# Fixing TensorE's order in the attention loop, and moving the preparation of six weight pieces into its first half

## The chip, the cores and the metric

The kernel runs on one core of a Trainium2 chip. The metric is device time in microseconds (us). Before the change it is 664.98 us, the median of three runs that lie between 664.54 and 666.16 us.

The engines go by the profile's names: PE is TensorE (matrix products and transposes), PEld its weight loads, DVE is VectorE, ACT is ScalarE, POOL is GpSimd, SP is SyncE, which here issues the DMAs.

## The reference

The program is an attention stage followed by two blocks on its result.

```
scores = q @ k.T / 8, kept where q and k have the same nearest centroid   # 2 batches x 8 heads, 768 x 768, depth 64
x = softmax(scores) @ v                                                   # -> [2, 768, 512]
h = relu(x.T @ w_tok1) @ w_tok2          # token weights: 768 x 256 and 256 x 768
u = x + h.T
x = u + relu(u @ w_ch1) @ w_ch2          # 512 -> 1536 -> 512
theta = x @ w_theta
y = w_tok_r @ (x * cos(theta)) + w_tok_i @ (x * sin(theta))
out = (x + y) + relu((x + y) @ w_ch)
```

Weights and the activations of the later blocks are split in a high and a low part, and a product takes three matmuls (L126, L127, L128).

## The kernel before

**Units.** Attention is 48 units: 16 heads times three pairs of 128-row query tiles. The loop at L485 issues in step n the scores of unit n, the turn of unit n-1 and the values of unit n-2.

- Scores (L380 to L407): eight matmuls, four for each of two query tiles, into one of two `ps_s` buffers a tile. DVE takes the negated row maximum (nm, L400), ACT the exponential (e, L402); this frees the `ps_s` buffer.
- Turn (L409 to L424): twelve 128 x 128 transposes into three `ps_t` tiles, the only three buffers that `ps_t` has. ACT copies two of them to SBUF (p, L420), DVE the third (L422).
- Values (L426 to L449): six matmuls, recorded in the trace as twelve, into `ps_o`, which has one buffer. ACT copies one half (tmp, L445), DVE adds the other (xt, L447); only then is the buffer free for the next unit's values.

**Work beside the units.** Six units are a pair of heads. For each next pair there are cluster masks (sim L246, pp L270, oh L271, m L286; sim and pp go through `ps_t`), and POOL splits the pair's q and k (`split_pair`: L346, L80, L86). After each pair `natural` (L451 to L467) turns its result into rows: six transposes x (L460) into two `ps_t` tiles, and six DVE products xn (L462). Below, an x-unit is a unit in which these x transposes stand.

**The six weight pieces.** `load_w` (L100 to L120) brings one piece of 128 x 512: a DMA on SP's queue, two ACT instructions (L109, L110), two on DVE (L112, L113), one on POOL (L116), and then the high part by POOL (L80) or ACT (L84) and the low part by POOL or DVE (L86). Its last argument names the engines: "pp" is POOL for both, "av" is ACT and DVE, "pv" POOL and DVE. w_tok1 has three pieces, issued in steps 41, 43 and 46 (`W1_AT`); w_tok2 has three, issued in step 48, behind the last tmp and p.

**Behind the attention** (called the tail here): `tok_up` of batch 0 (18 matmuls g for each of two halves, L126 to L128; then gh by ACT L147 and gl by DVE L148), the split of batch 1's rows (xh by ACT L84, xl by DVE L86), and `tok_down` of batch 0 (h, L126 to L128).

**What sets the order.** Every engine runs its queue in order. The queues are filled by a scheduler that simulates a timeline (L799) and picks among the instructions that are ready; `tc.issue_after(x)` adds that an instruction stands behind x in its own engine's queue. Where the program names no such order, the scheduler has interleaved scores, transposes and values of neighbouring units.

Of the kernel before, what the change touches and what calls it, by code (L numbers as in the profile page):

```python
# [31 lines left out]
HL = 4  # L32

X_AT = (29, 31, 33, 35, 37, 39)
W1_AT = {41: "pp", 43: "pp", 46: "av"}
PREP = (1, 0)
PACE = 2
TH0 = 6
# [11 lines left out]
def tile_model(ctx: ExitStack, tc: tile.TileContext, qT, kT, v, cent, w1, w2, wc1, wc2, wth, wri, wch, out):  # L50


    nc = tc.nc
    B, H, D, S = qT.shape
    NT = S // P
# [12 lines left out]
    marks = {}  # L68
# [61 lines left out]
    w1s, w2s, xs, gs = [], [], {}, {}  # L130
# [30 lines left out]
    with ExitStack() as actx:  # L161
# [218 lines left out]
        def scores(b, h, u, ops):  # L380

            qh, ql, k1, kk, _ = ops
            es = []
            for j in range(2):
                qt = 2 * u + j
                c = slice(qt * P, qt * P + P)
                ps = ps_s.tile([P, 2, 512], F32, tag="s", name=f"s{b}{h}{qt}")
                first = (b, h, u) == (0, 0, 0)
                if first:

                    for half in range(2):
                        nc.tensor.matmul(ps[:, half, :NH], qh[:, c], k1[:, half * NH : half * NH + NH], start=True, stop=False)
                with tc.issue_after(marks["cl"].ins) if first else nullcontext():
                    for half in range(2):
                        n = slice(half * NH, half * NH + NH)
                        if not first:
                            nc.tensor.matmul(ps[:, half, :NH], qh[:, c], k1[:, n], start=True, stop=False)  # L397
                        marks["scores"] = nc.tensor.matmul(ps[:, half, :NH], ql[:, c], kk[:, n], start=False, stop=True)  # L398
                nm = small.tile([P, 1], F32, tag="nm", bufs=4, name=f"nm{b}{h}{qt}")
                marks["max"] = nc.vector.tensor_reduce(out=nm, in_=ps[:, :, :NH], axis=AX.XY, op=ALU.max, negate=True)  # L400
                e = ap.tile([P, S], F32, tag="e", bufs=4, name=f"e{b}{h}{qt}")
                marks["exp"] = nc.scalar.activation(  # L402
                    out=e.rearrange("p (a n) -> p a n", a=2), in_=ps[:, :, :NH], func=AF.Exp,
                    bias=nm, accum_out=sums[b, h // 2][:, qt, h % 2 : h % 2 + 1],
                )
                es.append(e)
            return es  # L407

        def turn(b, h, u, es):  # L409

            pr = []
            for j in range(NT // 2):
                ps = ps_t.tile([P, 2, 256], F32, tag="t", name=f"t{b}{h}{u}{j}")
                for i in range(2):
                    for a in range(2):
                        kt = 2 * j + a
                        marks["turn"] = nc.tensor.transpose(ps[:, a, i * P : i * P + P], es[i][:, kt * P : kt * P + P], ident)  # L417
                p = ap.tile([P, 2, 256], F32, tag="p", bufs=PB, name=f"p{b}{h}{u}{j}")
                if KINDS[j] == "A":
                    marks["pA"] = nc.scalar.activation(out=p, in_=ps, func=AF.Copy)  # L420
                else:
                    marks["pV"] = nc.vector.tensor_copy(out=p, in_=ps)  # L422
                pr.append(p)
            return pr  # L424

        def values(us):  # L426


            if us[-1][0] == len(units) - 1:
                ps = ps_s.tile([P, 2, 512], F32, tag="s", name="olast")[:, 0, :]  # L430
            else:
                ps = ps_o.tile([P, 512], F32, tag="o", name=f"o{us[0][0]}")
            outs = []
            for i, (n, pr, vs) in enumerate(us):
                po = ps[:, 256 * i : 256 * i + 256]
                for kt in range(NT):
                    r = 64 * (kt % 2)
                    nc.tensor.matmul(  # L438
                        po[r : r + 64, :], vs[:, kt, :], pr[kt // 2][:, kt % 2, :], start=kt < 2, stop=kt >= NT - 2,
                        tile_position=(0, r),  # L440
                    )
                outs.append((units[n], po))
            for (b, h, u), po in outs:
                tmp = ap.tile([64, 256], F32, tag="tmp", bufs=2, name=f"tmp{b}{h}{u}")
                marks["tmp"] = nc.scalar.activation(out=tmp, in_=po[64:128, :], func=AF.Copy)  # L445
                r0 = 64 * (h % 2)
                nc.vector.tensor_tensor(  # L447
                    out=xts[b, h // 2][r0 : r0 + 64, u * 256 : u * 256 + 256], in0=po[0:64, :], in1=tmp, op=ALU.add
                )  # L449
# [25 lines left out]
        with tc.issue_after(marks["cst"].ins):  # L475
            ops = {heads[0]: prep_pair_first(raws) + (vs00,)}
# [5 lines left out]
        units = [(b, h, u) for b, h in heads for u in range(NT // 2)]  # L482
        es, prs = {}, {}
        late, group = [], []
        for n in range(len(units) + SKEW):  # L485
            if n < len(units):
                b, h, u = units[n]
                if u == 0 and h % 2 == 0:
                    sums[b, h // 2] = small.tile([P, NT, 2], F32, tag="sm", bufs=2, name=f"sm{b}{h}")
                    xts[b, h // 2] = ap.tile([P, S], F32, tag="xt", bufs=2, name=f"xt{b}{h}")  # L490
                if n != 1:
                    es[n] = scores(b, h, u, ops[b, h])
                if n == 0:
                    next(first, None)
                    place(1, ms[0, 0])
                    scored = marks["scores"]
                    es[1] = scores(*units[1], ops[b, h])
                    with tc.issue_after(marks["max"].ins):
                        ops[heads[1]] = prep_first(*heads[1])
                    marks["scores"] = scored  # L500
                    for w, k in zip(WARM[1:], ("cps", "sim", "scores")):
                        with tc.issue_after(marks[k].ins):
                            warm_up(w)
                h1 = n // 3 + 1
                if 1 < h1 < len(heads) and u == PREP[h1 % 2]:
                    b2, h2 = heads[h1]
                    ops[b2, h2] = prep(b2, h2, ms[b2, h2 // 2])
                p1 = n // 6 + 1
                if p1 < len(heads) // 2:
                    pr = heads[2 * p1][0], heads[2 * p1][1] // 2  # L510
                    if n % 6 == PAIR_AT[0]:
                        raws = load_pair(*pr)
                    if n % 6 == PAIR_AT[1]:
                        split_pair(*pr, raws)
                    if n % 6 == PAIR_AT[2]:
                        gen = masks(*pr)
            if n >= 3:
                for _ in range(PACE):
                    next(gen, None)
            if n == 42:  # L520
                mctx.close()
            if 0 <= n - 1 < len(units):
                prs[n - 1] = turn(*units[n - 1], es.pop(n - 1))
            if n < 3:
                with tc.issue_after((marks["turn"] if n else marks["scores"]).ins):
                    for _ in range(PACE):
                        next(gen, None)
            if 0 <= n - SKEW:
                b, h, u = units[n - SKEW]
                group.append((n - SKEW, prs.pop(n - SKEW), ops[b, h][4]))  # L530
                if len(group) == GROUP:
                    with tc.issue_after(marks["turn"].ins):
                        values(group)
                    group = []
                if h % 2 == 1 and u == NT // 2 - 1:
                    late.append((n + 1, b, h // 2))
            while late and (n >= late[0][0] or n == len(units) + SKEW - 1):
                _, b, pr = late.pop(0)
                natural(b, pr)
            if n in X_AT:  # L540
                tok_x(0, X_AT.index(n), part, "pp")
            if n in W1_AT:
                with tc.issue_after(marks["exp"].ins):
                    i = len(w1s)
                    w1s.append(load_w(w1[:, i * 512 : i * 512 + 512], f"w1_{i}", W1_AT[n]))
            if n == len(units):
                with tc.issue_after(marks["tmp"].ins), tc.issue_after(marks["pA"].ins), tc.issue_after(marks["pV"].ins):
                    for i in range(NT // 2):
                        w2s.append(load_w(w2[:, :, i * 256 : i * 256 + 256], f"w2_{i}", "pv"))


        ps = ps_s.tile([P, 2, 512], F32, tag="s", name="g0")
# [194 lines left out]
    for n in range(len(steps) + 2):  # L747
        if n < len(steps):
            t, b = steps[n]
# [53 lines left out]
```

## Time and profile before

| | |
|---|---|
| median of 3 runs | 664.98 us |
| the profiled execution's own time | 664.99 us |
| span of the profiled execution | 663.3 us |
| mean granted TensorE clock | 0.995 |
| PE busy | 646.8 us, 98% |
| DVE busy | 401.2 us, 60% |
| ACT busy | 344.9 us, 52% |
| POOL busy | 257.6 us, 39% |

The span runs from the first to the last instruction; 1.7 us of the execution lie outside it. Attention takes the first 245 us or so, the two blocks the rest. A start-to-start difference between two PE rows is the time that PE's queue really took for what lies between them; the busy time of a row is longer where matmuls overlap.

### The profile page before, as it was taken

The numbers are of one execution on the slowest core, as the hardware profiler recorded it, in microseconds if no ns is written. First come the engines' busy times: TensorE is split into PE (matmuls) and PEld (weight loads), VectorE is DVE, ScalarE is ACT, GpSimd is POOL, SyncE is SP. The second block draws the span as 40 slices with busy tenths as digits, with TensorE's granted clock in tenths as the row PEclk, the third lists the DMA queues.
The fourth block names the chain that finished last, engine by engine and source line by source line (L and its number), as shares of the span: only waits on it lengthen the run. The fifth ranks groups of instructions, "written<-read, shape, count | busy, mean of one in ns | idle before, by whom it ended". The sixth has DMA issues, their size and how long they took to land.

```text
span 663.3 us, 9795 instructions
## 1 busy us (share of the span) xinstructions
PE 646.8 (98%) x3591; PEld 517.7 (78%) x3591; DVE 401.2 (60%) x649; ACT 344.9 (52%) x653; POOL 257.6 (39%) x231
## 2 busy tenths in 40 slices
PE   7999999999999989999999999999999999999998
PEld 4777777777777758878888888888887878888886
DVE  5877778687787776466665442546677694531212
ACT  5676776777767863256444320428487673320000
POOL 6230312364031131138887520603467796541000
PEclk9999999999999998999999999999999999999999
DMA  8554755444555121023433310310021424300001
GB/s 294 160 138 105 169 123 144 120 117 114 113 123 124 37 96 47 18 67 124 154 133 127 126 53 14 95 33 0 1 85 42 128 88 127 114 20 33 16 33 47
DMA packets 24207, 61.42 MB, mean 93 GB/s; under 512 B 4256, under 2 KB 7520, under 8 KB 24160
## 3 DMA queue, kind: packets, MB, share of 16 engines
q1 hardware_dynamic: 24160, 60.80, 32.3%
q8 instruction: 28, 0.46, 0.3%
q14 instruction: 19, 0.16, 0.1%
HBM read 39.65 MB, written 3.15 MB: 65 GB/s over the span
## 4 chain that ended last, share of the span: by engine, by line
PE 86%; ACT 4%; DVE 3%; POOL 3%; issue 2%; DMA 2%; SPq 0%; POOLq 0%; ACTq 0%
PE o L438 10%; PE t L417 9%; PE s L397 5%; PE r L126 5%; PE r L127 5%; PE r L128 5%; PE c L126 5%; PE c L127 5%; PE c L128 5%; PE s L398 5%; PE y L128 4%; PE y L127 4%; PE y L126 4%; PE po L126 2%; PE po L128 2%
## 5 line engine op out<-in xcount | busy, mean ns | idle before, releaser
L402 ACT ACTIVATE e<-s,nm 128x768 f32<-128x768 f32 x96 | 86.7, 905 | 29.4 <-DVE nm L400 28.1
L400 DVE TENSOR_REDUCE nm<-s 128x1 f32<-128x768 f32 x96 | 90.5, 951 | 18.9 <-PE s L398 18.0
L417 PE MATMUL t<-ident,e 128*128 128x128 f32 x576 | 80.5, 275 | 0.6 <-ACT p L420 0.5
L417 PEld LDWEIGHTS t<-ident,e 128*128 128x128 f32 x576 | 66.4, 140 | 16.0 <-issue 9.4
L397 PE MATMUL s<-k,qh 128*128 128x384 f32 x188 | 71.9, 382 | 2.5 <-ACT e L402 2.3
L438 PE MATMUL o<-p,vs 128*64 128x256 f32 x564 | 71.2, 388 | 0.0
L398 PE MATMUL s<-k,q 128*128 128x384 f32 x192 | 65.3, 343 | 2.4 <-DVE q L279 2.4
L420 ACT ACTIVATE p<-t 128x512 f32<-128x512 f32 x96 | 52.2, 594 | 25.4 <-PE t L417 25.0
L126 PE MATMUL r<-ul,c_h 128*128 128x512 f32 x144 | 56.5, 396 | 0.4 <-DVE ul L90 0.4
L126 PE MATMUL y<-zl,k_h 128*128 128x512 f32 x144 | 56.1, 390 | 0.0
L128 PE MATMUL y<-zh,k_h 128*128 128x512 f32 x144 | 56.1, 390 | 0.0
L127 PE MATMUL r<-uh,c_l 128*128 128x512 f32 x144 | 56.1, 390 | 0.0
L127 PE MATMUL y<-zh,k_l 128*128 128x512 f32 x144 | 56.0, 389 | 0.0
L127 PE MATMUL c<-c_h,rl 128*128 128x512 f32 x144 | 56.0, 390 | 0.0
L128 PE MATMUL r<-uh,c_h 128*128 128x512 f32 x144 | 56.0, 390 | 0.0
L128 PE MATMUL c<-c_h,rh 128*128 128x512 f32 x144 | 55.9, 390 | 0.0
L126 PE MATMUL c<-c_l,rh 128*128 128x512 f32 x144 | 55.2, 391 | 0.0
L438 PEld LDWEIGHTS o<-p,vs 128*64 128x64 f32 x564 | 36.3, 136 | 22.7 <-issue 5.9
L116 POOL TENSOR_TENSOR c_f<-c_f,c_raw 128x512 uint32<-128x512 uint32 x24 | 31.6, 1318 | 44.7 <-issue 31.3
L80 POOL TENSOR_SCALAR qh<-ql 128x768 fp32r<-128x768 f32 x7 | 5.8, 835 | 100.9 <-DMA qh<-qh 100.8
L397 PEld LDWEIGHTS s<-k,qh 128*128 128x128 f32 x188 | 35.4, 188 | 11.1 <-ACT e L402 5.6
L398 PEld LDWEIGHTS s<-k,q 128*128 128x128 f32 x192 | 36.7, 192 | 3.8 <-ACT k L276 3.4
(192 smaller groups left out, 1387.9 us busy)
## 6 DMA issues: line engine op xcount, KB each, us to landing
c_raw<-wc SPq DMA_DIRECT2D x24, 512.0 KB, 3.3
k_raw<-wri SPq DMA_DIRECT2D x18, 512.0 KB, 3.5
qh<-qh SPq DMA_DIRECT2D x28, 192.0 KB, 3.0
k<-kh SPq DMA_DIRECT2D x28, 192.0 KB, 3.8
ql<-qT SPq DMA_DIRECT2D x8, 384.0 KB, 3.2
kl<-kT SPq DMA_DIRECT2D x8, 384.0 KB, 4.6
vs<-v SPq DMA_DIRECT2D x16, 192.0 KB, 2.4
w_raw<-w SPq DMA_DIRECT2D x6, 512.0 KB, 4.1
```

Source lines behind the costliest of these rows:

```text
L80: nc.gpsimd.tensor_scalar(out=h, in0=x, scalar1=1.0, scalar2=0.0, op0=ALU.mult, op1=ALU.add)
L116: nc.gpsimd.tensor_tensor(out=wu, in0=wu, in1=lo, op=ALU.add)
L126: nc.tensor.matmul(ps, ah, bl, start=first and i == 0, stop=False)
L127: nc.tensor.matmul(ps, al, bh, start=False, stop=False)
L128: nc.tensor.matmul(ps, ah, bh, start=False, stop=last and i == n - 1)
L397: nc.tensor.matmul(ps[:, half, :NH], qh[:, c], k1[:, n], start=True, stop=False)
L398: marks["scores"] = nc.tensor.matmul(ps[:, half, :NH], ql[:, c], kk[:, n], start=False, stop=True)
L400: marks["max"] = nc.vector.tensor_reduce(out=nm, in_=ps[:, :, :NH], axis=AX.XY, op=ALU.max, negate=True)
L402: marks["exp"] = nc.scalar.activation(out=e.rearrange("p (a n) -> p a n", a=2), in_=ps[:, :, :NH], func=AF.Exp, bias=nm, accum_out=sums[b, ...
L417: marks["turn"] = nc.tensor.transpose(ps[:, a, i * P : i * P + P], es[i][:, kt * P : kt * P + P], ident)
L420: marks["pA"] = nc.scalar.activation(out=p, in_=ps, func=AF.Copy)
L438: nc.tensor.matmul(po[r : r + 64, :], vs[:, kt, :], pr[kt // 2][:, kt % 2, :], start=kt < 2, stop=kt >= NT - 2, tile_position=(0, r),)
```

## The change

There are two parts. The first gives PE a fixed order in attention: the scores of unit n stand behind the last values matmul issued so far (unit n-3), and the transposes of unit n-1 stand behind the scores of unit n. The values stood behind the transposes already. The second issues the six weight pieces in steps 8, 12, 16, 20, 24 and 28, first the three of w_tok1, then those of w_tok2, each behind an exponential on ACT, and all with "pp".

```diff
-W1_AT = {41: "pp", 43: "pp", 46: "av"}
+W_AT = (8, 12, 16, 20, 24, 28)
...
-                    nc.tensor.matmul(
+                    marks["o"] = nc.tensor.matmul(
...
                 if n != 1:
-                    es[n] = scores(b, h, u, ops[b, h])
+                    with tc.issue_after(marks["o"].ins) if "o" in marks else nullcontext():
+                        es[n] = scores(b, h, u, ops[b, h])
...
-                prs[n - 1] = turn(*units[n - 1], es.pop(n - 1))
+                with tc.issue_after(marks["scores"].ins) if n > 2 else nullcontext():
+                    prs[n - 1] = turn(*units[n - 1], es.pop(n - 1))
...
-            if n in W1_AT:
+            if n in W_AT:
                 with tc.issue_after(marks["exp"].ins):
-                    i = len(w1s)
-                    w1s.append(load_w(w1[:, i * 512 : i * 512 + 512], f"w1_{i}", W1_AT[n]))
-            if n == len(units):
-                with tc.issue_after(marks["tmp"].ins), tc.issue_after(marks["pA"].ins), tc.issue_after(marks["pV"].ins):
-                    for i in range(NT // 2):
-                        w2s.append(load_w(w2[:, :, i * 256 : i * 256 + 256], f"w2_{i}", "pv"))
+                    i = W_AT.index(n)
+                    if i < NT // 2:
+                        w1s.append(load_w(w1[:, i * 512 : i * 512 + 512], f"w1_{i}", "pp"))
+                    else:
+                        i -= NT // 2
+                        w2s.append(load_w(w2[:, :, i * 256 : i * 256 + 256], f"w2_{i}", "pp"))
```

PE's queue in steps 10 and 11 of the loop, before. s034 and s035 are the scores of unit 11, t0310 to t0312 the transposes of unit 10, o8 the values of unit 8; "x2" is two instructions in a row.

```order
L397 MATMUL s034_871<-k103_568,qh03_567 128x384
L398 MATMUL s034_871<-k2_1_152,q2_1_150 128x384
L397 MATMUL s034_871<-k103_568,qh03_567 128x384
L398 MATMUL s034_871<-k2_1_152,q2_1_150 128x384
L438 MATMUL o8_861<-p0220_782,vs02_465 64x256 x2
L438 MATMUL o8_861<-p0221_789,vs02_465 64x256 x2
L438 MATMUL o8_861<-p0222_796,vs02_465 64x256 x2
L417 MATMUL t0310_889<-ident_61,e032_815 128x128 x2
L417 MATMUL t0311_896<-ident_61,e032_815 128x128 x2
L417 MATMUL t0312_903<-ident_61,e032_815 128x128 x2
L397 MATMUL s035_880<-k103_568,qh03_567 128x384
```

The same place of PE's queue after the change:

```order
L438 MATMUL o8_873<-p0222_808,vs02_465 64x256 x2
L397 MATMUL s034_883<-k103_568,qh03_567 128x384
L398 MATMUL s034_883<-k2_1_152,q2_1_150 128x384
L397 MATMUL s034_883<-k103_568,qh03_567 128x384
L398 MATMUL s034_883<-k2_1_152,q2_1_150 128x384
L397 MATMUL s035_892<-k103_568,qh03_567 128x384
L398 MATMUL s035_892<-k2_1_152,q2_1_150 128x384
L397 MATMUL s035_892<-k103_568,qh03_567 128x384
L398 MATMUL s035_892<-k2_1_152,q2_1_150 128x384
L417 MATMUL t0310_901<-ident_61,e032_827 128x128 x2
L417 MATMUL t0310_901<-ident_61,e033_836 128x128 x2
```

The values moved ahead of both score tiles, and the transposes no longer stand between the two score tiles.

DVE's queue in unit 17 (query tiles s054 and s055), before. o14 are the values of unit 14, p0502 and p0512 the third copies of the turns of units 15 and 16.

```order
L400 TENSOR_REDUCE nm053_1195<-s053_1190 128x1
L422 COPY p0502_1232<-t0502_1227 128x512
L400 TENSOR_REDUCE nm054_1249<-s054_1244 128x1
L447 TENSOR_TENSOR xt04_921<-o14_1234,tmp042_1241 64x256
L400 TENSOR_REDUCE nm055_1258<-s055_1253 128x1
L422 COPY p0512_1281<-t0512_1276 128x512
```

The same unit after; w1_2 is the third piece of w_tok1.

```order
L400 TENSOR_REDUCE nm053_1219<-s053_1214 128x1
L422 COPY p0502_1256<-t0502_1251 128x512
L400 TENSOR_REDUCE nm054_1285<-s054_1280 128x1
L112 TENSOR_SCALAR w1_2_raw_1268<-w1_2_f_1270 128x512
L400 TENSOR_REDUCE nm055_1294<-s055_1289 128x1
L447 TENSOR_TENSOR xt04_933<-o14_1258,tmp042_1265 64x256
L113 SCALAR_TENSOR_TENSOR w1_2_f_1270<-w1_2_f_1270,w1_2_raw_1268 128x512
L422 COPY p0512_1317<-t0512_1312 128x512
```

The piece's two DVE instructions came in, and the addition xt, which frees `ps_o`, moved from between the two maxima to behind both.

ACT's queue behind the last tmp (the tail), before. gh00 and gh01 are the two halves of `tok_up` of batch 0, xh10 to xh15 the six tiles of batch 1, w2_2 the last piece of w_tok2, c1_0 the first of the next block's weights.

```order
L147 ACTIVATE gh00_3286<-g0_3267 128x512
L109 ACTIVATE w2_2_f_3230<-w2_2_raw_3228 128x512
L84 ACTIVATE xh10_3312<-xn6_72 128x512
L84 ACTIVATE xh11_3316<-xn7_73 128x512
L147 ACTIVATE gh01_3308<-g0_3267 128x512
L84 ACTIVATE xh12_3320<-xn8_74 128x512
```

The same place after:

```order
L147 ACTIVATE gh00_3286<-g0_3267 128x512
L84 ACTIVATE xh10_3312<-xn6_72 128x512
L84 ACTIVATE xh11_3316<-xn7_73 128x512
L84 ACTIVATE xh12_3320<-xn8_74 128x512
L84 ACTIVATE xh13_3324<-xn9_75 128x512
L84 ACTIVATE xh14_3328<-xn10_76 128x512
L84 ACTIVATE xh15_3332<-xn11_77 128x512
L109 ACTIVATE c1_0_f_3598<-c1_0_raw_3596 128x512
L110 ACTIVATE c1_0_raw_3596<-c1_0_raw_3596 128x512
L147 ACTIVATE gh01_3308<-g0_3267 128x512
```

The second half's gh01 moved from behind two of the six xh to behind all six and behind two instructions for c1_0. From there on the queues of all engines hold the same instructions in the same order before and after.

## Rows read from the trace of the kernel before

**Rows 1.** The page, busy time of TensorE (us, share of the span, instructions).

```profile
PE 646.8 (98%) x3591; PEld 517.7 (78%) x3591; DVE 401.2 (60%) x649; ACT 344.9 (52%) x653; POOL 257.6 (39%) x231
```

**Rows 2.** The chain of waits through attention: start, duration (us), what; values only.

```profile
51.87 1.45 PE o L438 x12
58.64 1.45 PE o L438 x12
62.97 1.45 PE o L438 x12
...
108.04 1.45 PE o L438 x12
...
202.76 1.45 PE o L438 x12
...
235.37 1.45 PE o L438 x12
```

**Rows 3.** Timeline of PE, a unit already in the new order: start, duration, instruction.

```profile
139.28 0.47 PE L397 MATMUL s<-k,qh 128*128 128x384 f32 x1
...
140.80 1.47 PE L417 MATMUL t<-ident,e 128*128 128x128 f32 x12
142.20 1.52 PE L438 MATMUL o<-p,vs 128*64 128x256 f32 x12
```

**Rows 4.** Timeline of all engines in an x-unit; brackets: idle time before, and releaser.

```profile
109.42 0.44 PE L397 MATMUL s<-k,qh 128*128 128x384 f32 x1
...
110.42 0.96 DVE L400 TENSOR_REDUCE nm<-s 128x1 f32<-128x768 f32 x1 [1.65 <-PE s L398]
...
111.63 1.26 DVE L462 TENSOR_TENSOR xn<-x,ri 128x128 f32<-128x128 f32 x6
...
112.52 0.44 PE L397 MATMUL s<-k,qh 128*128 128x384 f32 x1 [0.62 <-ACT e L402]
...
113.28 1.80 DVE L400 TENSOR_REDUCE nm<-s 128x1 f32<-128x768 f32 x2
```

**Rows 5.** Timeline of all engines where a weight piece is prepared in attention.

```profile
217.49 0.69 ACT L109 ACTIVATE w_f<-w_raw 128x512 f32<-128x512 f32 x1
...
218.66 0.42 DVE L112 TENSOR_SCALAR w_raw<-w_f 128x512 uint32<-128x512 uint32 x1
...
220.12 0.42 DVE L447 TENSOR_TENSOR xt<-o,tmp 64x256 f32<-64x256 f32 x1
...
220.57 0.69 DVE L113 SCALAR_TENSOR_TENSOR w_f<-w_f,w_raw 128x512 uint32<-128x512 uint32 x1
```

**Rows 6.** Timeline of the tail, all engines.

```profile
245.77 0.60 ACT L147 ACTIVATE gh<-g 128x512 fp32r<-128x512 f32 x1 [2.34 <-PE g L128]
245.78 1.69 DVE L86 TENSOR_TENSOR w_l<-w_f,w_h 128x512 fp32r<-128x512 f32 x2
...
247.79 0.68 DVE L148 SCALAR_TENSOR_TENSOR gl<-g,gh 128x512 fp32r<-128x512 f32 x1
...
248.52 0.50 PE L126 MATMUL g<-xl,w_h 128*128 128x512 f32 x1 [2.57 <-DVE gl L148]
...
249.06 0.63 ACT L84 ACTIVATE xh<-xn 128x512 fp32r<-128x512 f32 x1 [1.49 <-PE g L126]
...
254.34 0.39 PE L126 MATMUL h<-gl,w_h 128*128 128x512 f32 x1
```

**Rows 7.** Windows: stretch; its length, busy PE, PEld, DVE, ACT, POOL; PEclk, DMA share, GB/s.

```profile
250.00:252.00 2.00, 2.00 (x6) 1.51 (x6) 0.19 (x1) 0.63 (x1) 1.69 (x2) 0.50 0.00 0
...
500.00:520.00 20.00, 18.36 (x89) 14.99 (x88) 15.48 (x24) 13.59 (x25) 15.43 (x13) 1.00 0.25 79
```

**Rows 8.** Timelines of POOL and DVE: a pair's split, and a weight piece in the tail.

```profile
157.44 1.84 POOL L86 TENSOR_TENSOR kl<-kl,kh 128x768 fp32r<-128x768 f32 x1 [0.51 <-DMA k<-kl]
...
241.74 1.33 POOL L116 TENSOR_TENSOR w_f<-w_f,w_raw 128x512 uint32<-128x512 uint32 x1 [7.24 <-DVE w_f L113]
...
241.96 1.67 DVE L113 SCALAR_TENSOR_TENSOR w_f<-w_f,w_raw 128x512 uint32<-128x512 uint32 x1
```

## The prediction

> **What bounds the kernel now.** I read the page's busy times first: TensorE is busy 98% of the span [rows 1], so time goes only where its queue gets shorter, stands still or runs at the lower clock. Then the chain of waits: through attention it runs almost wholly over TensorE's own matmuls. From one unit's values to the next one's is 62.97 - 58.64 = 4.33 us where nothing else is done, and 58.64 - 51.87 = 6.77 us in a unit with an x transpose and a mask [rows 2]. Third, the timeline of one unit that the scheduler of before happened to lay down in the new order: scores 139.28 to 140.80 (1.52), transposes to 142.20 (1.40), values 1.45, together 4.37 us [rows 3]. Attention is paced by TensorE, and the other engines count only where they make it stop. The places where it stops are few: an x-unit, 0.62 us of waiting for an exponential [rows 4]; the pieces prepared in attention; and the tail, where it stands 2.57 us before the second set of g matmuls and then runs at half clock for a while [rows 6, 7]. Since the queues behind the tail are the same in both kernels, the change is won or lost in attention and tail. Four terms follow. The profiled execution took 664.99 us, its span 663.3 (so 1.7 outside it), and the median of the runs is 664.98; I apply the sum to the latter.
>
> **Tail (A).** The second g set waits for gl of the first half. Its gh ends at 245.77 + 0.60 = 246.37, but gl starts at 247.79: two w_l of the last pieces and two xn stand ahead of it on DVE [rows 6]. After the change the w_l are gone; the two xn should be through when gh ends. So gl can start at about 246.4, 1.4 us earlier, and the idle time falls from 2.57 to about 1.2: -1.4. Second, the clock: 250 to 252 us has a granted clock of 0.50, that is 1.2 of 2.4 GHz, right behind that long idle time [rows 7]. The 18 g matmuls took 254.34 - 248.52 = 5.82 us [rows 6]. At full clock a 128x512 matmul takes 0.23 us from start to start (89 in 20 us is 0.225 [rows 7]), 18 of them 4.15: -1.7 if the clock stays up. I take it that it stays, since 500 to 520 keeps a clock of 1.00 although 1.64 us of it are idle [rows 7]. Third, a loss: gh of the second half now stands on ACT behind six xh and c1_0's two instructions. An xh can only start when the g matmuls of its row tile are through, so the sixth ends about 4.5 us after the g set starts; then 2 x 0.69 [rows 5], gh 0.60 and gl 0.68 [rows 6], near 7.0. The matmuls that need only the first half last until 4.15 + 9 x 0.23 = 6.2: +0.8. A = -1.4 - 1.7 + 0.8 = -2.3. Bounds: -4.2 (all idle and slow time goes, gh comes in time) and +0.8 (nothing of either goes).
>
> **Pieces no longer at the end of attention (B).** From 202.76 to 235.37 are 32.61 us [rows 2]: seven units at 4.35 make 30.45, six x transposes half a turn, 0.70, one score tile that fell into this stretch 0.76 [rows 3]. The 0.70 us left are what the three pieces cost there: -0.7 (between 0 and -1.2). The three of w_tok2 are in term A.
>
> **Pieces in units 9, 13, 17, 21, 25, 29 (C).** What each issues: a DMA, two ACT instructions of 0.69, L112 0.42 and L113 0.69 on DVE [rows 5], three on POOL. Two things are hidden. POOL is busy 39% [rows 1], a piece is needed only after 245 us, and what is behind it there, a pair's split, has units to spare. The DMA passes through SP's queue between the pairs' loads, which are also issued units ahead; 512 KB at once could delay a pair, and if that cover failed a unit would wait for its operands, once, for up to a unit's 4.35 us; I do not see it coming, since the loads are asked for up to six units ahead. ACT is not the limit either: 1.4 us fit beside its two exponentials and two copies in most units. DVE is where it hurts, because values must wait for xt of the unit before (`ps_o` has one buffer). Take unit 17, with zero at its first score matmul. The first maximum starts at 1.00 (110.42 - 109.42 [rows 4]) and a maximum takes 0.90 (two in 1.80 [rows 4]): it ends at 1.90. Without the piece xt comes next and ends at 2.32, before TensorE is through with scores and transposes at 1.52 + 1.40 = 2.92. In the new queue L112 (to 2.32), the second maximum (to 3.22) and xt (0.42, to 3.64) follow. The values start 0.72 late. Unit 29 has the same order: 0.7. Unit 13, which has L112 and L113 among a mask's instructions: about 0.65. Units 9 and 21 are x-units, where both stand among xn and oh: 1.11 us of work into a queue that has some wait in it, 0.6 each. Unit 25 has its xt ahead of the piece: 0. C = 0.7 + 0.7 + 0.65 + 0.6 + 0.6 = +3.3. Bounds: 0, if the real order of arrivals lets xt pass everywhere, and 6 x 1.11 = +6.7, if all DVE work of the pieces lands on the path. I take the middle, the row-by-row count.
>
> **The fixed order (D).** What it removes: the interleaving. The plain unit was 4.33 and is 4.37 when pinned [rows 2, 3], since each switch between kinds costs a little; with a part of the units already in that order I take 0.03 for 40 units, +1.2 (0 to +1.6). x-units: before, 0.62 us of idle time in every other pair, three in all [rows 4]; it can go, because both score tiles now start directly after the values. In its place the transposes follow the scores at once and need `ps_t` buffers which the x tiles and pp hold until six xn (1.26 [rows 4]) are done; I take this as an even exchange, 0, with -1.9 (three stalls vanish) and +2.5 (four more of 0.62) as ends. D = +1.2, from -1.9 to +4.1.
>
> **Sum.** -2.3 - 0.7 + 3.3 + 1.2 = +1.5: 664.98 + 1.5 = 666.5 us. A difference under 0.3%, 2.0 us, can't be told from no change here, so the forecast is "the same", 663.0 to 667.0.
>
> **Rivals.**
>
> 1. The pieces hide. DVE has 40% of its time free, and if xt gets through in time in most units C is 0.3, and the pinned order costs nothing: -2.3 - 0.7 + 0.3 + 0 = -2.7, 662.3 us. For it: in before, three pieces in a row in attention cost 0.70 together, not 0.7 each. Against it: there xt stood ahead of L113 [rows 5], and here it stands behind. Chance 0.27.
>
> 2. Slower: DVE and GpSimd get in each other's way. L113 takes 0.69 in [rows 5] but 1.67 when it starts at 241.96 while GpSimd's L116 (241.74, 1.33) runs; it ends some 0.6 after it [rows 8]. In attention GpSimd runs the pair splits, 1.84 us an instruction [rows 8], and now the low parts of six pieces. If L113 or L112 meets one, it is about 1 us longer, and with it the xt or the maximum behind it. It decides when this falls on units with no slack, 13 and 25, which come just behind the splits, and one more: +2.5, 669.0 us. Chance 0.13.
> The Trainium skill, SBUF — State Buffer, section "Who interferes with whom", speaks for this rival: a VectorE instruction with two SBUF inputs contends with a GpSimd instruction that reads SBUF, and whoever comes second waits for the whole instruction. The trace agrees, with 1.67 for 0.69. By that rule every L113 (two inputs) that meets a split would lose up to 1.84 us; six times would be +11 us, which I hold for out of reach, as GpSimd is idle most of the time.
>
> 3. The clock falls in the tail in spite of the shorter idle time: the -1.7 of A is lost, 668.2 us. For it: 1.2 us of idle time is left. Chance 0.07.
>
> 4. ACT becomes the loop. With the fixed order each unit's second score tile waits for an exponential two tiles back; the way from scores over maximum (0.90), exponential and ACT's copies to the next scores is near the unit's 4.37, by some 0.2. If it is 0.1 over in 44 units: +4.4, 670.9 us. Against it: the pinned unit of [rows 3] shows no wait between its instructions. Chance 0.06.
>
> **How the numbers follow.** The forecast has the remaining 0.47, its own range is 664.7 to 668.3. Faster by over 0.3% (under 663.0): most of rival 1, 0.21, and 0.01 of the forecast, 0.22. Slower (over 667.0): rivals 2 to 4, 0.26, and 0.10 of the forecast, 0.36. The same: 0.36 of the forecast and 0.06 of rival 1, 0.42. The range for 8 in 10 takes in the centre of rival 1 nearly and of rival 2 whole: 662.5 to 669.5; outside it lie rival 4, half of rival 1 below 662.3 and the tail of rival 2.
>
> **What would show it right or wrong.** A: idle time before the second g set of 1.2 us, no window at clock 0.50 behind it, and a wait of under 1 us for gl of the second half before the tenth h matmul. C: in units 17 and 29, values that wait 0.7 us for xt with L112 ahead of it; in unit 25 none. D: values starts 4.37 apart in plain units, and no wait for an exponential in x-units but one for xn or oh. The forecast is wrong if the distance from values to values in the six units is no longer than in their neighbours (rival 1), if L113 in attention shows durations above 1 us (rival 2), or if score tiles wait for exponentials in every unit (rival 4).

## The result, and the profile after

The changed kernel takes 669.97 us (median of five runs, 669.35 to 671.60); the kernel before, with two more runs, takes 665.99. The ratio on record is 1.0070, with a 95% interval of 1.0048 to 1.0092: slower by some 4.6 us (the two medians alone differ by 4.0), outside the predicted range and on the side that I gave 0.36. The profiled execution took 669.75 us with a span of 667.9, 4.6 more than in the trace of before.

The page of the changed kernel first: the busy times, and two groups of instructions (busy us, mean ns | idle time before them, and what ended most of it).

```profile
PE 644.7 (97%) x3591; PEld 517.7 (78%) x3591; DVE 403.3 (60%) x645; ACT 341.7 (51%) x652; POOL 264.9 (40%) x236
...
L417 PE MATMUL t<-ident,e 128*128 128x128 f32 x576 | 72.3, 273 | 3.9 <-DVE xn L462 3.7
L438 PE MATMUL o<-p,vs 128*64 128x256 f32 x564 | 71.2, 388 | 3.7 <-DVE xt L447 3.7
```

TensorE's busy time fell from 646.8 [rows 1], yet the span grew, so TensorE stands still more. The two groups say where: transposes wait for xn, and values for xt. Neither was among the waits of before; its page has

```profile
L417 PE MATMUL t<-ident,e 128*128 128x128 f32 x576 | 80.5, 275 | 0.6 <-ACT p L420 0.5
L438 PE MATMUL o<-p,vs 128*64 128x256 f32 x564 | 71.2, 388 | 0.0
```

The values' starts in the timeline give the account. I take three marks: the first values, the values of unit 39 (the fortieth; the expectations below write "up to unit 40"), and the first matmul of the last unit's values (`olast`). The end of h is the start of the matmul behind it.

| stretch | before | after | difference |
|---|---|---|---|
| span's start to first values | 24.05 | 23.61 | -0.44 |
| to unit 39's values | 182.24 | 189.34 | +7.10 |
| to `olast` | 32.86 | 31.75 | -1.11 |
| to the end of h | 23.34 | 21.47 | -1.87 |
| to the span's end | | | +0.96 |

The sum is 4.64, against 667.9 - 663.3 = 4.6. The loss lies in the middle of attention, between these rows, two of before and then two of after:

```profile
24.05 1.51 PE L438 MATMUL o<-p,vs 128*64 128x256 f32 x12
...
206.29 1.52 PE L438 MATMUL o<-p,vs 128*64 128x256 f32 x12
```

```profile
23.61 1.51 PE L438 MATMUL o<-p,vs 128*64 128x256 f32 x12
...
212.95 1.52 PE L438 MATMUL o<-p,vs 128*64 128x256 f32 x12
```

Its largest part is in unit 13, by the timeline of all engines. A unit is named by its scores; the values in it are two units older.

```profile
70.40 1.52 PE L438 MATMUL o<-p,vs 128*64 128x256 f32 x12
...
72.63 0.44 PE L397 MATMUL s<-k,qh 128*128 128x384 f32 x1
...
72.87 1.85 POOL L86 TENSOR_TENSOR kl<-kl,kh 128x768 fp32r<-128x768 f32 x1 [0.37 <-DMA k<-m]
...
73.30 1.71 DVE L112 TENSOR_SCALAR w_raw<-w_f 128x512 uint32<-128x512 uint32 x1
...
74.12 1.47 PE L417 MATMUL t<-ident,e 128*128 128x128 f32 x12
...
75.39 0.94 DVE L400 TENSOR_REDUCE nm<-s 128x1 f32<-128x768 f32 x1
...
76.06 0.83 POOL L346 TENSOR_SCALAR ql<-ql 128x768 f32<-128x768 f32 x1 [1.34 <-DMA ql<-qT]
76.25 1.18 DVE L113 SCALAR_TENSOR_TENSOR w_f<-w_f,w_raw 128x512 uint32<-128x512 uint32 x1
...
77.46 0.42 DVE L447 TENSOR_TENSOR xt<-o,tmp 64x256 f32<-64x256 f32 x1
...
77.93 0.87 PE L438 MATMUL o<-p,vs 128*64 128x256 f32 x6 [2.33 <-DVE xt L447]
```

From values to values are 77.93 - 70.40 = 7.53 us, where a unit with a mask takes 5.13 (units 7 and 37): 2.40 lost. Units 19 and 31, which have a mask and no piece either, take 5.35 in this kernel; against them it is 2.18. L112 took 1.71 instead of 0.42 while GpSimd's kl ran (it ends 0.29 after it), L113 1.18 instead of 0.68 beside the next split. That is 1.29 + 0.50 = 1.79 of it; the other 0.4 to 0.6 is left for the piece's two instructions themselves, which both stand ahead of xt here. Unit 17 shows a loss without any stretching:

```profile
92.42 1.51 PE L438 MATMUL o<-p,vs 128*64 128x256 f32 x12
...
95.74 0.42 DVE L112 TENSOR_SCALAR w_raw<-w_f 128x512 uint32<-128x512 uint32 x1
...
96.07 0.95 DVE L400 TENSOR_REDUCE nm<-s 128x1 f32<-128x768 f32 x1
...
96.94 0.41 DVE L447 TENSOR_TENSOR xt<-o,tmp 64x256 f32<-64x256 f32 x1
97.27 0.68 DVE L113 SCALAR_TENSOR_TENSOR w_f<-w_f,w_raw 128x512 uint32<-128x512 uint32 x1
97.40 1.51 PE L438 MATMUL o<-p,vs 128*64 128x256 f32 x12 [0.57 <-DVE xt L447]
```

The values start right behind xt; from the unit before (92.42) that is 4.98, 0.63 over a plain unit's 4.35. The tail, which answers to [rows 6]:

```profile
251.39 0.60 ACT L147 ACTIVATE gh<-g 128x512 fp32r<-128x512 f32 x1 [2.42 <-PE g L128]
...
252.09 0.69 DVE L148 SCALAR_TENSOR_TENSOR gl<-g,gh 128x512 fp32r<-128x512 f32 x1
...
252.83 0.50 PE L126 MATMUL g<-xl,w_h 128*128 128x512 f32 x1 [1.32 <-DVE gl L148]
...
253.43 4.05 ACT L84 ACTIVATE xh<-xn 128x512 fp32r<-128x512 f32 x6 [1.44 <-PE g L126]
...
257.04 0.39 PE L126 MATMUL h<-gl,w_h 128*128 128x512 f32 x1
...
258.50 0.58 ACT L147 ACTIVATE gh<-g 128x512 fp32r<-128x512 f32 x1
...
259.91 0.50 PE L126 MATMUL h<-gl,w_h 128*128 128x512 f32 x1 [0.67 <-DVE gl L148]
```

The idle time is 1.32 instead of 2.57, the 18 g matmuls take 257.04 - 252.83 = 4.21 instead of 5.82, and h waits for the second half's gl behind the six xh: 9.13 for 36 matmuls instead of 8.16.

### The profile page after: what moved, and what is told of

It is laid out like the page before. It is cut to its first block, busy times and chain, and to the rows that moved or that the text cites. A ratio compares the mean times of both kernels' runs of the same rounds, so it can differ in the third digit from the quotient of the medians.

```text
span 667.9 us, 9852 instructions
## 1 busy us (share of the span) xinstructions
PE 644.7 (97%) x3591; PEld 517.7 (78%) x3591; DVE 403.3 (60%) x645; ACT 341.7 (51%) x652; POOL 264.9 (40%) x236
## 5 line engine op out<-in xcount | busy, mean ns | idle before, releaser
L417 PE MATMUL t<-ident,e 128*128 128x128 f32 x576 | 72.3, 273 | 3.9 <-DVE xn L462 3.7
L397 PE MATMUL s<-k,qh 128*128 128x384 f32 x188 | 69.7, 371 | 1.8 <-ACT e L402 1.7
L420 ACT ACTIVATE p<-t 128x512 f32<-128x512 f32 x96 | 53.6, 595 | 27.0 <-PE t L417 26.8
L653 DVE TENSOR_TENSOR xn<-c,xn 128x512 f32<-128x512 f32 x36 | 24.4, 686 | 25.1 <-PE c L128 25.0
```

Source lines behind the costliest of these rows:

```text
L653: nc.vector.tensor_tensor(out=xn[t], in0=ps, in1=xn[t], op=ALU.add)
```

## The experiments

In each, the ratio is to the kernel before on the same chip, with its 95% interval; 0.001 is 0.67 us. The changed kernel stands at 1.0070. e1_pin to e8_free ran on one chip, e9_free_xn, e10_xunits and b2_before_again on another, on which the kernel before takes 664.08 instead of some 665.1 us.

**e1_pin, the fixed order alone.** The edit is the change without its second part:

```diff
+                    with tc.issue_after(marks["o"].ins) if "o" in marks else nullcontext():
+                        es[n] = scores(b, h, u, ops[b, h])
...
+                with tc.issue_after(marks["scores"].ins) if n > 2 else nullcontext():
+                    prs[n - 1] = turn(*units[n - 1], es.pop(n - 1))
```

> Only TensorE's fixed order; the weight pieces are issued where they were before. Theory 1 (the fixed order itself costs: every plain unit 4.35 instead of 4.32, and every x-unit waits about 0.7 for xn before its transposes, where before only every other one lost about 1.0): 2 to 3 us slower than before, values-to-values in x-units about 5.75, tail as before (2.57 idle, then the slow clock). Rival (the order is free, all of the loss comes from the pieces): within 1 us of before, x-units 5.1 as the short ones of before.

Measured: 669.60 us, ratio 1.0067 (1.0047 to 1.0088). Up to unit 39's values it is 3.25 us behind the kernel before, and a further 1.28 to `olast`, where the pieces of w_tok1, which stand in this kernel as before, meet the fixed order. An x-unit of it, on TensorE and VectorE:

```profile
165.59 1.52 PE L438 MATMUL o<-p,vs 128*64 128x256 f32 x12
...
168.04 0.96 DVE L400 TENSOR_REDUCE nm<-s 128x1 f32<-128x768 f32 x1 [1.36 <-PE s L398]
...
168.92 0.41 DVE L447 TENSOR_TENSOR xt<-o,tmp 64x256 f32<-64x256 f32 x1
...
169.25 1.26 DVE L462 TENSOR_TENSOR xn<-x,ri 128x128 f32<-128x128 f32 x6
...
170.26 1.50 PE L417 MATMUL t<-ident,e 128*128 128x128 f32 x12 [0.74 <-DVE xn L462]
...
171.69 1.52 PE L438 MATMUL o<-p,vs 128*64 128x256 f32 x12
```

It takes 171.69 - 165.59 = 6.10, 1.07 over a plain unit with its x and pp matmuls (5.03). All six x-units up to unit 40 read alike: 6.4 us. The same sum over the x-units of before is 3.2 (0.98, 0.08, 0.98, 0.08, 0.98, 0.08, counted without the half unit of scores that the long ones take in advance). So +3.2 comes from x-units and next to nothing, 0.05, from all plain units together: these take 4.35 each, and the 4.31 of before is made up by a 4.36 elsewhere. Theory 1 named the right place and the wait (0.74), but it had x-units of 5.75, which take 6.10, and a total of 2 to 3 us, which is 4.5 by the ratio. The rival's short x-units of 5.1 did not come. The tail is as expected, with 2.57 us of idle time and then the slow clock once more (18 g matmuls in 5.70 us; columns as in [rows 7]):

```profile
253.00:255.00 2.00, 2.00 (x6) 1.52 (x6) 0.55 (x1) 0.98 (x2) 1.22 (x1) 0.50 0.00 0
```

**e2_pieces, the pieces alone.** The edit is `W_AT` with its `load_w` calls, and no order on TensorE.

> Only the six pieces moved to steps 8 to 28 with both parts by GpSimd; TensorE's order is free. Theory 1 (pieces cost by themselves what they hold up on VectorE): 5 us in attention, 0.7 and 1.9 given back at its end and in the tail, so 1.5 to 2.5 us slower than before, and 2 to 3 faster than the whole change. Rival (pieces cost only because the fixed order leaves no room for a late xt): faster than before by 1.5 to 2.5.

Measured: 666.97 us, ratio 1.0025 (1.0011 to 1.0039), within theory 1. The longest L112 and L113 are 1.92 and 2.33 us here, in the same two places beside the splits; the pieces hurt without the fixed order too. The two parts alone add up to 1.0092, the change measures 1.0070, a difference within the intervals. The traces show an overlap: up to unit 39's values the parts lose 3.25 and 6.08, the change 7.10. That an x-unit which waits for xn hides a piece (e10_xunits) is one reason; that it is the only one is not shown.

**e3_shift, other steps.** One line, to steps that are not beside a split:

```diff
-W_AT = (8, 12, 16, 20, 24, 28)
+W_AT = (10, 16, 22, 28, 34, 40)
```

> The whole change, but with the pieces in steps 10, 16, 22, 28, 34, 40, none of which falls beside a pair's split on GpSimd, and all of which have the queue of unit 17 on VectorE (maximum, L112, maximum, xt). Theory 1 (the 2.40 of unit 13 and 0.7 of unit 25 are VectorE and GpSimd getting in each other's way): no L112 or L113 in attention above 0.75, each of the six values late by 0.63, 3.8 together instead of 5.0, and about 1 to 1.5 us faster than the whole change. Rival (a late transpose and maximum of the mask do it, whatever GpSimd does): some of the six units lose over 1 us again, no change in time.

Measured: 668.82 us, ratio 1.0054 (1.0037 to 1.0072). Every one of the six values starts 0.63 late, to the hundredth. The duration of L112 (ns: least, median, most), first after the change, then here:

```profile
L112 DVE TENSOR_SCALAR w_raw<-w_f x6: 417/418/1711, 54.5 to 154.2; 128x512 uint32<-128x512 uint32 x6
```

```profile
L112 DVE TENSOR_SCALAR w_raw<-w_f x6: 416/418/419, 64.8 to 210.5; 128x512 uint32<-128x512 uint32 x6
```

Without a split beside it the instruction never stretches, nor does L113 (674 to 680 ns), and the large loss is gone. The drop in time, 0.0016, is within the intervals, and in the traces it is 0.65 us up to unit 39's values (188.69 instead of 189.34); the durations carry this verdict.

**e4_xt, xt ahead of the piece.** Two edges on VectorE, in the units that have a piece:

```diff
-                marks["max"] = nc.vector.tensor_reduce(...)
+                with tc.issue_after(marks["xt"].ins) if j and u0 in W_AT else nullcontext():
+                    marks["max"] = nc.vector.tensor_reduce(...)
...
-                with tc.issue_after(marks["exp"].ins):
+                with tc.issue_after(marks["exp"].ins), tc.issue_after(marks["xt"].ins):
```

> The whole change, with two more edges on VectorE: in the six units a piece's two instructions, and the second maximum, stand behind xt. Theory 1 (the values wait because xt is late behind L112 and the maximum): values in units 17 and 29 no longer late (0.63 each gone), unit 13 loses under 1 instead of 2.4, in all 2 to 3.5 us faster than the whole change. Rival (VectorE is simply too full in these units): the wait moves to the next scores or transposes and the time stays within 1 us of the whole change.

Measured: 665.08 us, ratio 1.0003 (0.9988 to 1.0018), 4.5 us faster than the change. Unit 17 again (lines behind 400 stand two higher in this kernel):

```profile
93.50 0.42 DVE L449 TENSOR_TENSOR xt<-o,tmp 64x256 f32<-64x256 f32 x1
93.84 0.41 DVE L112 TENSOR_SCALAR w_raw<-w_f 128x512 uint32<-128x512 uint32 x1
94.18 0.94 DVE L402 TENSOR_REDUCE nm<-s 128x1 f32<-128x768 f32 x1
...
94.31 0.87 PE L440 MATMUL o<-p,vs 128*64 128x256 f32 x6
```

xt ends at 93.92, before TensorE is ready, and the values wait no more (4.35 from the unit before). Units 17 and 29 lose nothing, and unit 13 takes the 5.35 of units with a mask and no piece: L112 now starts when GpSimd's kl is just over. So in unit 13 the meeting with kl went as well, and e4_xt does not tell it from the new place of xt. Up to unit 39's values the trace is 5.0 us shorter (184.34), more than theory 1 forecast. The same work on VectorE, in another order, costs some 4 to 5 us less, so VectorE was not too full.

**e5_shift_xt, both.** The steps of e3_shift with the edges of e4_xt.

> The pieces in steps 10, 16, ... 40 as in e3_shift, with the two VectorE edges of e4_xt (piece and second maximum behind xt). Theory 1 (each of the six values is late by 0.63 because xt stands behind L112 and the maximum): all six waits go, 3.8 us faster than e3_shift, about 665. Rival (part of it is lack of room on VectorE): some 0.3 of each stays, 666.5 to 667.

Measured: 665.50 us, ratio 1.0000 (0.9987 to 1.0012). From the first values to unit 39's it takes 184.80 us against 188.69 in e3_shift: 3.89 for six waits of 0.63 (3.78). This settles the size of a piece's cost and its cause.

**e10_xunits, pieces in x-units.** The whole change with `W_AT = (8, 14, 20, 26, 32, 38)`.

> The whole change, but the six pieces in steps 8, 14, 20, 26, 32, 38, so that each falls into an x-unit, away from GpSimd's splits and with the queue that unit 9 had. Theory 1 (in an x-unit TensorE waits for xn anyway, and a piece there costs nothing: unit 9 took 6.11 with the piece and 6.10 without; the 2.40, 0.63, 0.49 and 0.63 of units 13, 17, 25 and 29 are what the pieces cost): every x-unit 6.1, no other unit late, 4 us less than the whole change in the stretch up to unit 40 apart from x-units at 1.07 instead of 0.71, so 667 to 668. Rival (the working of the prediction, 0.6 for a piece in an x-unit): x-units of 6.7, 669 to 671.

Measured: 666.36 us, ratio 1.0033 (1.0021 to 1.0046), 2.5 us faster than the change, as theory 1 said. An x-unit with a piece:

```profile
80.98 1.52 PE L438 MATMUL o<-p,vs 128*64 128x256 f32 x12
...
84.31 0.42 DVE L112 TENSOR_SCALAR w_raw<-w_f 128x512 uint32<-128x512 uint32 x1
...
84.64 1.27 DVE L462 TENSOR_TENSOR xn<-x,ri 128x128 f32<-128x128 f32 x6
...
85.66 1.50 PE L417 MATMUL t<-ident,e 128*128 128x128 f32 x12 [0.75 <-DVE xn L462]
...
87.09 1.08 PE L438 MATMUL o<-p,vs 128*64 128x256 f32 x8
```

6.11 with the piece, 6.10 without [e1_pin]; the unit behind it is 0.08 longer. L112 takes the place that xt had between the maximum and xn, xt goes behind, and since the transposes wait for xn anyway, the late xt still comes before the values. The prediction's 0.6 for such a unit was wrong.

**e6_tail, gh ahead of xh.** e4_xt, and in the tail:

```diff
+        with tc.issue_after(marks["gh"].ins):
             for s in range(NT):
                 tok_x(1, s, part, "av")
```

> e4_xt, and in the tail gh of the second half stands ahead of the six xh on ScalarE. Theory 1: the 0.97 us that the h matmuls waited for it (36 of them in 9.14 instead of 8.16) goes, 664.1 us. Rival: batch 1's xh are now late for the next g matmuls, and these wait instead; no change.

Measured: 665.21 us, ratio 1.0007 (0.9990 to 1.0024). In the trace the 36 h matmuls take 8.32 instead of 9.14, and the next g set starts without a wait, so the term is real; in the time it can't be seen.

**e7_x, x ahead of the scores.** e6_tail, and in the unit behind each pair the scores stand behind all x transposes and the first maximum behind the six xn.

```diff
+                    with tc.issue_after(marks["x" if n - 1 in nats else "o"].ins) ...
+                        es[n] = scores(b, h, u, ops[b, h])
...
+                with tc.issue_after(marks["xn" if u0 in nats else "xt"].ins) if u0 in nats or (j and u0 in W_AT) else nullcontext():
```

> e6_tail, and in the unit behind each pair the scores stand behind all six x transposes on TensorE and the first maximum behind the six xn on VectorE. Theory 1 (the fixed order costs because transposes directly behind the scores wait for the buffers that x holds until xn, 0.7 to 1.07 in each of seven x-units): 0.2 or less in each, 3 to 4.5 us faster than e6_tail, 660 to 661. Rival (the mask's pp and oh hold the third buffer and the maximum is now late): the wait stays above 0.5, within 1 us of e6_tail.

Measured: 664.30 us, ratio 0.9977 (0.9957 to 0.9996). The x-units lose 0.36 to 0.57 instead of 0.39 to 1.06, the stretch from the first values to `olast` falls from 216.03 to 214.10. Half of what theory 1 promised; the other half turned into another wait, here in an x-unit:

```profile
168.47 1.04 PE L419 MATMUL t<-ident,e 128*128 128x128 f32 x8
169.76 0.66 PE L419 MATMUL t<-ident,e 128*128 128x128 f32 x4 [0.25 <-ACT p L422]
170.35 0.87 PE L440 MATMUL o<-p,vs 128*64 128x256 f32 x6
```

The last transposes wait for ScalarE's copy p of the first, as pp still holds the third buffer until oh.

**e8_free and e9_free_xn, the order free again.** e6_tail without the fixed order; then with the first maximum behind xn as well.

> e6_tail without TensorE's fixed order: pieces in steps 8 to 28 with the edges on VectorE, gh ahead of xh. Theory 1 (the fixed order costs 2.5 us up to unit 40 in x-units and plain units, and the pieces' cost is xt standing late): 2 us faster than e6_tail, about 662. Rival (without the fixed order the pieces collide with interleaved scores whatever xt does): slower than e6_tail, 665 to 666.

> e8_free (order of TensorE free, pieces behind xt, gh ahead of xh) and the first maximum behind the six xn in the unit behind each pair. Theory 1 (the remaining 0.9 in the long x-units is the wait of scores for an exponential whose maximum is late): with xn ahead the maximum is later still, and the long x-units stay at 6.6 or more; no change or up to 1 us slower. Rival (xn late is what matters, as in the fixed order): x-units fall to 5.4, 2 us faster than e8_free, about 661.5.

Measured: e8_free 663.54 us, ratio 0.9976 (0.9962 to 0.9989); e9_free_xn 665.47, ratio 1.0022 (1.0007 to 1.0036). By the ratios e8_free is 2 us faster than e6_tail, which only adds the fixed order, as theory 1 said. In the traces it is 1.1 us up to `olast` (214.94 instead of 216.03), and 0.9 and not 2.5 up to unit 39's values, so the rest of the 2 us has no place in the traces. e8_free and e7_x are the two versions whose intervals lie below the kernel before. e9_free_xn answers to neither expectation. Of the long x-units (6.57, 6.73 and 6.75 in e8_free) two fell to 5.88, but the 5.88 no longer holds scores taken in advance (some 0.75), and one stayed at 6.73. The short ones rose (5.32, 5.31 and 5.11 to 5.64, 5.64 and 5.89), and the scheduler laid nearly all plain units down in the slower pattern (4.36 instead of 4.31).

**b2_before_again.** No edit.

> The kernel before once more, for a second trace. In the first one the c matmuls that follow the last of w_ch1's pieces start without a wait, and in the changed kernel and all seven variants they lose 0.8 to 1.1 us there. If the wait belongs to the changed attention, it is missing here too; if it comes and goes between executions of one kernel, it may show here.

Measured: 662.82 us, span 661.1. The wait at the c matmuls showed with some 0.5 us, so it can come without the changed attention. The trace has something else, in the tail (columns of the window: length, busy PE, PEld, DVE, ACT, POOL, then the granted clock, DMA share, GB/s):

```profile
248.91 0.50 PE L126 MATMUL g<-xl,w_h 128*128 128x512 f32 x1 [2.54 <-DVE gl L148]
```

```profile
250.00:252.00 2.00, 2.00 (x11) 1.65 (x10) 0.00 (x0) 0.72 (x2) 1.75 (x2) 1.00 0.00 0
```

Nearly the same idle time as in [rows 6], 2.54 us, and the clock stays at 1.00 where it was 0.50 in [rows 7] and in e1_pin; the 18 g matmuls take 4.21. This trace is from another chip than e1_pin's; whether that matters is not tested.

## Why the prediction was wrong

The sum failed by 3.1 us against the ratio's 4.6, and these are its terms.

**The fixed order (D), predicted +1.2, measured +3.25 in e1_pin up to unit 39's values.** The step that failed is "I take this as an even exchange, 0": the transposes' wait for xn in x-units costs 1.07 each time, six times, where the scheduler had paid 0.98 every other time and 0.08 otherwise. I had the mechanism, and priced it by the interruption that it replaced and not by its own chain, which the rows gave: maximum, xt and six xn in a row, begun at 1.00 [rows 4], end 1.00 + 0.90 + 0.42 + 1.26 = 3.58 us after the first score matmul, when scores, x and pp have been through since some 2.2 (1.52 + 0.68). The other half of D was wrong too: 0.03 for 40 plain units was read from a single pair of units, and came to 0.05 in all. Nor does the reason given for it fit, that each switch between kinds of matmul costs a little: the unit of before from 62.90 to 67.20 us has five stretches of one kind and takes 4.30, a unit in the fixed order has three and takes 4.35.

**The pieces (C), predicted +3.3, measured +3.9 to +4.4.** The lower figure takes units 13 and 25 against 5.35, the higher against 5.13; what is left of the 7.10 for D is then 3.2 or 2.7. Units 17 and 29: 0.7 predicted, 0.63 measured, by the chain that I gave; e4_xt and e5_shift_xt take it away, so that mechanism is shown. Units 9 and 21: 0.6 predicted, 0 measured against the 6.10 of e1_pin, since the x-unit's own wait covers them (e10_xunits). Unit 13: 0.65 predicted, 2.18 to 2.40 measured. Unit 25: 0 predicted, 0.49 to 0.70 measured, of which 0.49 in the unit behind it. Here the step that failed is that the forecast's count let no piece meet a split. These two are rival 2, in the units that it named: L112 1.71 and L113 1.18 and 1.26 beside splits. Taken by the ratio (664.98 + 4.6), the rival's time, 669.0, was the nearest of all. Luck has a part in that, as D's miss made up for the 1.2 that units 9 and 21 did not cost. Its chance, 0.13, was too low: the steps 12 and 24 are multiples of six, when a pair is split, and this could have been laid side by side before. I thought of the stretch as falling on L113 alone, as in [rows 8]; it fell most on L112. By the Trainium skill, SBUF — State Buffer, section "Who interferes with whom", a one-input VectorE instruction in a two-port mode takes the shared port as well, and the loser waits for the whole instruction. The trace agrees: L112 ends 0.29 us after the kl that it met. Whether L112 runs in such a mode, no row here tells.

**The end of attention (B), predicted -0.7, measured -1.1.** Near, but in part by luck: with the pieces left there the fixed order alone adds 1.28 to this stretch (e1_pin), and taking them away gives back 2.39 (34.14 to 31.75), not 0.7.

**The tail (A), predicted -2.3, measured -1.87.** Idle time -1.25 (-1.4 predicted), clock -1.61 (-1.7), gh behind xh +0.97 (+0.8). Each step came as it was worked out; the terms of the last one (4.5, twice 0.69, 0.60 and 0.68) add up to 7.16 and not to "near 7.0", and give the +0.96 that was measured. But the clock term does not belong to every execution: of three traces with the long idle time two have it (before and e1_pin), the second trace of before has not. Against that one A would be about -0.3. The mean granted clock, which is on record for every run, speaks for the change: it is 0.995 or less in 74 of 80 runs of the kernel before and in 41 of 104 runs of the kernels with the shorter idle time. But a mean does not say where the clock fell (the second trace of before has 0.995 too), so how much of the 1.6 us the change gives back on average stays open. The bound of +0.8 allowed for its loss; the middle of the forecast counted it whole.

**The rest.** -0.44 before the first values and +0.96 behind the tail were not predicted. The first differs between executions (23.5 to 25.2 in these traces). The second lies almost wholly in one wait of c matmuls for rl, while the last weights of that block are prepared. From start to start it is 0.8 to 1.0 in the changed kernel and all its variants, 0.5 in one trace of before and none in the other. Why it is larger there stays open.

Rival 1 (pieces hidden) did not happen as it stands but is reachable for the pieces: e4_xt. Its time of 662.3 was not reached (e4_xt 665.08). Rival 3 (the clock falls in spite of the shorter idle time) and rival 4 (ScalarE becomes the loop) did not happen: plain units take 4.35 and wait for nothing.

## What to carry to other kernels

A fixed order of the bounding engine is worth what its irregular units are worth: check those in which other work holds the buffers before counting the regular ones. Work that an idle-looking engine takes on costs when it stands ahead of the one short instruction that frees a single buffer; put that instruction first, and the same work is nearly free. When moved VectorE work can meet GpSimd, lay the two engines' periods side by side: here one meeting cost 1.8 us, and moving the pieces to steps away from the splits removed it.

## What the runs showed of the hardware

An L112 of 0.42 us took 1.71 beside GpSimd's kl, and 1.92 in e2_pieces; an L113 of 0.68 took up to 2.33. Over all traces one regularity lets such a meeting be priced: a piece's L112 that was stretched ended 0.28 to 0.32 us after the GpSimd instruction that it met, an L113 0.53 to 0.56 us after it; where L112 or L113 started first it kept its usual time (L112 0.42 beside a kl that began 0.12 us later, in the changed kernel).

After an idle time of 2.54 to 2.57 us the granted clock was 0.50 in two executions (before, e1_pin) and 1.00 in a third (b2_before_again), worth 1.6 us. A shorter idle time can come ahead of it too: in e7_x TensorE stood 0.57 and 1.24 us shortly before this stretch,

```profile
544.00:546.00 2.00, 2.00 (x6) 1.55 (x5) 1.97 (x4) 1.12 (x2) 2.00 (x3) 0.50 0.82 238
```

and in e4_xt, with 0.52 and 1.22 us at the same place, the clock stayed at 1.00. Between runs of one kernel the times differ by up to 0.9% (e6_tail: 663.61 to 669.79), so a trace's total says less than its stretches.
